# A search loop with its count turned on VectorE, its next choice moved into the gather, and transposes spread among products

## The chip, the cores and the metric

The kernel runs on one core of one Trainium2 chip. The metric is the time of one execution on the device in microseconds; of several runs the median is taken. The profile is of one more execution of the same program, taken by the hardware profiler.

## What is computed

The reference joins two blocks. The first is a linear attention without a softmax over 8 batches, 8 heads, 576 positions and head size 64: for each batch and head `kv = k^T v`, then `out = q kv`, divided by its root mean square over the head's 64 elements and scaled by `g_norm`. Its result is laid out as 4608 tokens of 512 elements.

The second is a mixture of 8 experts with a balanced choice. Each token has 8 logits (`x @ w_gate`). The pairs of token and expert are taken in falling order of their logits; a pair is granted if the token has no expert yet and the expert has fewer than 576 tokens. Then each expert computes `relu(x @ w1[e]) @ w2[e]` for its 576 tokens (512 to 1024 to 512 elements), and the rows go back to the tokens' places. All of it is float32.

## The kernel before

**Attention, lines 269 to 424.** The work goes batch by batch, two batches' loads ahead. Besides the outputs, each token's 8 logits and its inverse norm per head are computed; the tokens are written to a DRAM buffer `x_dram` (rows of 8 x 72 float32: a head's 64 elements, then the inverse norm and the logits). The logits lie in `lg`, [128 partitions, 8 experts, 36 columns]. `early` (269) makes the first choice and the first comparison for the columns as they become ready.

**The balanced choice, lines 234 to 262 and 437 to 542.** It is done in eight turns. In each turn one expert becomes full and is then computed. `choose` (234) finds each token's best open expert: `mx` is the logit, `best` a 0/1 tensor in bfloat16 that marks the expert. `threshold` (437) searches the logit at which the first expert becomes full: seven steps, each of which divides an interval into 33 parts. A step (i) makes 32 candidate levels (`candidates`, 259), (ii) compares every `mx` with each of them (`compare`, 254; `over` is [128, 36, 32]), (iii) counts, for each candidate and expert, the tokens above it: nine products on TensorE (`n_ps`, 453), each of four columns' `over` with the same columns' `best`, of whose result the four diagonal blocks are added on VectorE (459), (iv) decides for each candidate whether some expert is full (463, 466), (v) counts those candidates over the partitions with a product with ones (`k_ps`, 469), which puts the number on all 128 partitions, and (vi) picks the two candidates that bound the next interval (474, twice). `assign` (478) then settles who goes to the full expert. `fetch` (548) reads the expert's number on the SP engine, issues the loads of `w1` (two halves of 1 MB) and `w2` (2 MB), finds the row numbers of the 576 tokens (`a_ps`, `s_ps`, `ids`), gathers the tokens in five blocks with indirect DMAs on GpSimd (`xg`, 588) and works out the output rows (`outs`, 603). `later` (523) closes the expert. The last expert takes the rest (532).

**The experts, lines 619 to 677.** `turn` (619) scales the gathered tokens with the inverse norms on VectorE (`xs`, 625), transposes each block with four transposes on TensorE (629) and copies the result to `xt` on ScalarE (630); the buffers of `xs` and of the PSUM tile are two. `layers` (640) does the first layer in 16 groups of 288 tokens (four products each, 652; a float32 product stands as two records in the trace) and the second layer in five blocks of tokens, the last with 64 tokens (eight products, 663; 671).

**What sets the order.** TensorE, VectorE and ScalarE run in the order in which the program is written out; generators are interleaved by hand in lines 679 to 698. While `layers(t)` is written out, `control(t + 1)` is advanced: it yields how many microseconds of products, by the program's own numbers (0.487 for a first-layer product, 0.858 for a second-layer one), shall stand before its next TensorE instructions. When `layers` reaches its last block, the rest of `control` and the whole `turn(t + 1)` are written out.

## Time and profile before

| | us |
|---|---|
| Median of three runs | 751.49 |
| The three runs | 751.44, 751.49, 753.72 |
| The profiled execution | 748.19 |
| Its span, first to last instruction | 746.4 |
| TensorE busy with matmuls | 651.8 |
| VectorE busy | 352.6 |
| ScalarE busy | 162.9 |
| GpSimd busy | 92.9 |

All times inside the trace are counted from the start of the span; 748.19 is the span and 1.8 us around it. PE is TensorE's matmuls, PEld its weight loads, DVE VectorE, ACT ScalarE, POOL GpSimd, SP the engine that issues the loads; L469 is line 469. In a timeline a row has the start, the length to the end of the last of its instructions, engine, line, operation, output<-inputs, shapes (output<-input) and the number of instructions put together; in brackets stands the idle time before it and what ended that. In a table of groups the number behind the x counts instructions, then come busy us, the mean length of one in ns, and the engine's idle time before them. A matmul's length holds its way through the array, so the starts of successive ones are closer than their lengths. In a table of stretches the granted TensorE clock follows the engines, as a share of 2.4 GHz, then the busy share of the DMA engines and GB/s.

### The profile page before, as it was taken

Reading aid. Unit: us, or ns where it says so; the run is one execution under the profiler, and the core shown is the slowest. Engines: PE = TensorE matmul, PEld = TensorE weight load, DVE = VectorE, ACT = ScalarE, POOL = GpSimd, SP = SyncE. Lnnn points to the kernel's source line nnn. Section 1 sums busy time; section 2 is a strip of 40 time slices with the busy share of each in tenths; the row PEclk is TensorE's granted clock in tenths of the full one; section 3 lists DMA queues with packets and bytes.
Section 4 is the critical chain, followed back from the end, with each engine's and each line's share of the span. In section 5 each row is a group of like instructions: output and inputs, shape, how many; then the busy total and the mean of one; then the engine's idle time right before and its main releaser. Section 6 shows DMA issues by size and latency. Waiting matters only on the chain.

```text
span 746.4 us, 12251 instructions
## 1 busy us (share of the span) xinstructions
PE 651.8 (87%) x5001; PEld 412.3 (55%) x5001; DVE 352.6 (47%) x1253; ACT 162.9 (22%) x331; POOL 92.9 (12%) x113
## 2 busy tenths in 40 slices
PE   4788786114999999999999999999999999999994
PEld 3666674103764576457546744774476457547741
DVE  3444666785456465555645563655365542010000
ACT  1544555001110211031112112210211022122100
POOL 0100100002002300410040004001300322010011
PEclk9968996555999999999999999999999999999998
DMA  8997897017005400720090027004500638010001
GB/s 283 307 305 253 288 344 295 32 40 257 1 1 185 176 1 0 277 83 1 15 324 22 1 77 277 8 0 150 206 6 1 239 122 297 14 43 7 1 28 35
DMA packets 41399, 93.34 MB, mean 125 GB/s; under 512 B 3456, under 2 KB 3456, under 8 KB 41344
## 3 DMA queue, kind: packets, MB, share of 16 engines
q1 hardware_dynamic: 34752, 72.49, 27.8%
q0 software_dynamic: 5888, 20.06, 7.5%
q8 instruction: 39, 0.64, 0.3%
q10 hardware_dynamic: 704, 0.02, 0.1%
q14 instruction: 16, 0.13, 0.1%
HBM read 72.50 MB, written 20.05 MB: 124 GB/s over the span
## 4 chain that ended last, share of the span: by engine, by line
issue 60%; PE 19%; POOL 10%; DVE 6%; DMA 2%; ACT 1%; ACTq 0%; POOLq 0%; DVEq 0%
POOL out_dram L634 5%; PE h_ps L652 5%; POOL xg L588 5%; PE o_ps L359 3%; PE qt_ps L290 3%; PE kv_ps L302 3%; PE y_ps L663 2%; DVE over L255 1%; DMA gw<-in_moe_w_gate_dram 1%; DMA xg<-x_dram,ids 1%; PE w_ps L329 1%; PE n_ps L453 1%; DVE need L459 0%; DVE kv L310 0%; DVE at L474 0%
## 5 line engine op out<-in xcount | busy, mean ns | idle before, releaser
L652 PE MATMUL h_ps<-xt,w_sb 128*128 128x288 f32 x1024 | 272.2, 417 | 0.0
L663 PE MATMUL y_ps<-w_sb,hid 128*128 128x512 f32 x512 | 227.2, 597 | 0.0
L652 PEld LDWEIGHTS h_ps<-xt,w_sb 128*128 128x128 f32 x1024 | 189.6, 191 | 52.5 <-issue 5.7
L663 PEld LDWEIGHTS y_ps<-w_sb,hid 128*128 128x128 f32 x512 | 94.8, 190 | 105.2 <-issue 104.3
L655 ACT ACTIVATE hid<-h_ps 128x288 f32<-128x288 f32 x128 | 52.5, 410 | 221.4 <-PE h_ps L652 221.4
L634 POOL DMA_INDIRECT out_dram<-y_sb,outs x40 | 40.9, 1022 | 453.5 <-ACT y_sb L666 403.1
L625 DVE TENSOR_TENSOR xs<-xg 128x512 f32<-128x512 f32 (+1 forms) x40 | 27.1, 690 | 90.3 <-PE t_ps L629 45.8
L255 DVE TENSOR_TENSOR over<-mx,cand 128x1152 bf16<-128x1152 f32 (+3 forms) x52 | 67.5, 1298 | 1.6
L666 ACT COPY y_sb<-y_ps 128x512 f32<-128x512 f32 x32 | 18.7, 585 | 209.2 <-PE y_ps L663 209.2
L676 DVE TENSOR_TENSOR y_sb<-y_ps,y_part 64x512 f32<-64x512 f32 x8 | 5.5, 683 | 95.4 <-ACT y_part L675 95.4
L588 POOL DMA_INDIRECT xg<-x_dram,ids x40 | 38.9, 972 | 73.3 <-DVE at_row L598 37.0
L453 PEld LDWEIGHTS <-over 128*128 128x128 bf16 x441 | 18.1, 97 | 38.5 <-DVE over L255 19.7
L629 PE MATMUL t_ps<-ident,xs 128*128 128x128 f32 (+1 forms) x160 | 23.9, 284 | 16.6 <-DVE xs L625 13.0
L359 PE MATMUL o_ps<-kvx,qt 64*64 64x72 f32 x1152 | 33.4, 264 | 5.7 <-issue 4.9
L474 DVE SCALAR_TENSOR_TENSOR at<-row_f,k_ps,cand 128x33 f32<-128x33 f32 x98 | 21.5, 257 | 34.3 <-PE k_ps L469 34.3
L453 PE MATMUL n_ps<-best,over 128*128 128x32 bf16 x441 | 19.2, 178 | 20.9 <-DVE cand L447 12.5
L630 ACT ACTIVATE xt<-t_ps,g_col 128x512 f32<-128x512 f32 (+1 forms) x40 | 24.4, 646 | 51.8 <-PE t_ps L629 51.6
L459 DVE TENSOR_TENSOR need<-goal,n_ps 32x8 f32<-32x8 f32 x49 | 7.5, 154 | 58.5 <-PE n_ps L453 58.5
L290 PE MATMUL qt_ps<-ident,q_sb 128*128 128x128 f32 x144 | 30.5, 340 | 5.2 <-ACT kvt L323 2.0
L302 PE MATMUL kv_ps<-v_sb,k_sb 64*64 64x64 f32 x1152 | 28.6, 245 | 7.3 <-issue 7.3
L359 PEld LDWEIGHTS o_ps<-kvx,qt 64*64 64x64 f32 x1152 | 27.4, 164 | 11.7 <-issue 10.0
L367 DVE TENSOR_REDUCE ms<-sq 128x8 f32<-128x512 f32 x36 | 24.2, 681 | 18.4 <-ACT sq L365 18.4
(162 smaller groups left out, 472.8 us busy)
## 6 DMA issues: line engine op xcount, KB each, us to landing
w_sb<-in_moe_w_dram SPq DMA_DIRECT2D x16, 1024.0 KB, 6.2
w_sb<-in_moe_w_dram SPq DMA_DIRECT2D x8, 2048.0 KB, 16.2
k_sb<-in_k_dram SPq DMA_DIRECT2D x16, 576.0 KB, 6.1
v_sb<-in_v_dram SPq DMA_DIRECT2D x16, 576.0 KB, 5.8
q_sb<-in_q_dram SPq DMA_DIRECT2D x16, 576.0 KB, 4.8
x_dram<-o_sb SPq DMA_DIRECT2D x16, 576.0 KB, 4.1
x_dram<-o_sb SPq DMA_DIRECT2D x4, 288.0 KB, 3.4
xg<-x_dram,ids POOLq DMA_INDIRECT x40
```

The costliest lines, as they stand in the source:

```text
L255: nc.vector.tensor_tensor(over[:, c0:c1], mx[:, c0:c1].rearrange("p (c o) -> p c o", o=1).to_broadcast([P, c1 - c0, NCAND]), cand[:, 1:NCA ...
L290: nc.tensor.transpose(t_ps[:, x, :], q_sb[:, (4 * n + x) * P:(4 * n + x + 1) * P], ident)
L302: nc.tensor.matmul(kv_ps[cs, l, r * D:(r + 1) * D], lhsT=k_sb[ls, r, j, :], rhs=v_sb[ls, r, j, :], start=(j < 2), stop=(j >= R - 2))
L359: nc.tensor.matmul(o_ps[n * HP:(n + 1) * HP, rp, (2 * r2 + l) * W:(2 * r2 + l + 1) * W], lhsT=turned_q[bn][ks, block // 2, l * HP:(l + 1) ...
L453: nc.tensor.matmul(n_ps, lhsT=over[:, c:c + G].rearrange("p c n -> p (c n)"), rhs=best[:, c:c + G].rearrange("p c e -> p (c e)"), start=(c ...
L588: nc.gpsimd.indirect_dma_start(out=xg[0:nr].rearrange("p h w -> p (h w)"), out_offset=None, in_=x_dram, in_offset=bass.IndirectOffsetOnAxi ...
L625: nc.vector.tensor_tensor(xs[0:nr].rearrange("p (h d) -> p h d", h=H), xg[0:nr, :, 0:D], xg[0:nr, :, D:D + 1].to_broadcast([nr, H, D]), op ...
L630: nc.scalar.mul(xt[:, :, a:a + nr], t_ps[:, :, 0:nr], g_col)
L634: put = nc.gpsimd.indirect_dma_start(out=out, out_offset=bass.IndirectOffsetOnAxis(ap=ids_of[t][0:nr, n:n + 1], axis=0), in_=y_sb[0:nr, :] ...
L652: nc.tensor.matmul(h_ps, lhsT=w1[:, 2 * (d % 2) + d // 2, f * P:(f + 1) * P], rhs=xt[:, d, cs], start=(d == 0), stop=(d == DC - 1))
L655: nc.scalar.activation(hid[:, f, cs], h_ps, ACT.Relu)
L663: nc.tensor.matmul(y_ps, lhsT=hid[:, f, a:a + nr], rhs=w2[:, f, :], start=(f == 0), stop=(f == FC - 1))
```

## The change

- In `threshold`, the steps of the first search keep `k_ps`, but the lower end is picked first, the next candidates and the comparison follow, and then the upper end is picked. In all later searches `k_ps` is gone: the 0/1 decisions of 32 candidates are spread over 64 columns, turned in two 32 x 32 blocks on VectorE into `some_t` (which holds an added column of one and of zero), and summed there, which gives the count plus one and the count on 32 partitions; these are turned into the two ends directly and written to four groups of 32 partitions. The upper end is then limited by the one before.
- `best` is laid out as [expert, column]; `choose` writes it and `assign` reads it in a row, and the moving side of `n_ps` reads four columns of each expert.
- `choose` and the first comparison of the next search move from the start of `control` to the end of the one before, behind the issue of the gather (for the first expert, behind its `turn`).
- `turn` is advanced block by block: the first two blocks are scaled ahead; the transposes of four blocks stand after every second product of the second layer's fourth block, those of the fifth in the middle of the last block.
- The first expert's `w2` load waits for the last gather of its tokens.
- The yields are new numbers.

```diff
     away = asg.tile([P, NSTEP, NCAND + 1], FT, name="away")
+    part_of = [((1.0 + 2.0 ** -18) / (NCAND + 1)) ** (s + 1) for s in range(NSTEP)]
     for s in range(NSTEP):
         nc.vector.tensor_scalar(away[:, s], in0=row_f[:, 0:NCAND + 1], scalar1=span,
-                                scalar2=((1.0 + 2.0 ** -18) / (NCAND + 1)) ** (s + 1), op0=AL.mult, op1=AL.mult)
+                                scalar2=part_of[s], op0=AL.mult, op1=AL.mult)
+    some_t = asg.tile([QP, 2, QP + 1], FT, name="some_t")
+    nc.vector.memset(some_t[:, 0, QP:QP + 1], 1.0)
+    nc.vector.memset(some_t[:, 1, QP:QP + 1], 0.0)
     room = asg.tile([P, E], FT, name="room")
...
     pick = asg.tile([P, E, GC], FT, name="pick")
-    best = asg.tile([P, GC, E], BF, name="best")
+    best = asg.tile([P, E, GC], BF, name="best")
     mx = asg.tile([P, GC], FT, name="mx")
...
         nc.vector.tensor_reduce(code_mx[:, cs], pick[:, :, cs].rearrange("p e c -> p c e"), axis=AXX, op=AL.max)
-        nc.vector.tensor_tensor(best[:, cs].rearrange("p c e -> p e c"), pick[:, :, cs], bc_c(code_mx[:, cs]),
+        nc.vector.tensor_tensor(best[:, :, cs], pick[:, :, cs], bc_c(code_mx[:, cs]),
                                 op=AL.is_equal)
...
-    def threshold(first):
+    def threshold(first, over):
         lo, hi = bottom, top
+        cand = cand0
         for s in range(NSTEP):
-            if first and s == 0:
-                cand, over = cand0, over0
-            else:
-                cand = candidates(s, lo)
-                over = asg.tile([P, GC, NCAND], BF, name="over", tag="over", bufs=2)
-                compare(over, cand)
-                nc.vector.tensor_copy(cand[:, NCAND + 1:NCAND + 2], hi)
-            yield 7.2 if s == 0 else 2.8
-            n_ps = bank([P, G * E], "n_ps")
+            yield 0.4 if s == 0 else 4.6
+            lo_was = lo
+            n_ps = bank([P, E, G], "n_ps")
             for c in range(0, GC, G):
                 nc.tensor.matmul(n_ps, lhsT=over[:, c:c + G].rearrange("p c n -> p (c n)"),
-                                 rhs=best[:, c:c + G].rearrange("p c e -> p (c e)"),
+                                 rhs=best[:, :, c:c + G],
                                  start=(c == 0), stop=(c == GC - G))
...
                 less = small("need", E)[0:QP]
-                nc.vector.tensor_tensor(less, need, n_ps[g * QP:(g + 1) * QP, g * E:(g + 1) * E], op=AL.subtract)
+                nc.vector.tensor_tensor(less, need, n_ps[g * QP:(g + 1) * QP, :, g], op=AL.subtract)
                 need = less
...
             n_full = small("n_full")[0:QP]
-            nc.vector.scalar_tensor_tensor(full, in0=n_ps[0:QP, 0:E], scalar=0.0, in1=need, op0=AL.add,
+            nc.vector.scalar_tensor_tensor(full, in0=n_ps[0:QP, :, 0], scalar=0.0, in1=need, op0=AL.add,
                                            op1=AL.is_ge, accum_out=n_full)
-            some = small("some", dt=BF)[0:QP]
-            nc.vector.tensor_scalar(some, in0=n_full, scalar1=0.5, scalar2=None, op0=AL.is_gt)
-            yield 1.4
-            k_ps = bank([P, 1], "k_ps")
-            nc.tensor.matmul(k_ps, lhsT=ones_b[0:QP, :], rhs=some, start=True, stop=True)
+            hi_was = hi
             ends = small("ends", 2)
             hi, lo = ends[:, 0:1], ends[:, 1:2]
-            for n in range(2):
+            def pick_end(n):
                 at = small("at", NCAND + 1)
...
                                                op0=AL.is_equal, op1=AL.mult, accum_out=ends[:, 1 - n:2 - n])
+            if first:
+                some = small("some_b", dt=BF)[0:QP]
+                nc.vector.tensor_scalar(some, in0=n_full, scalar1=0.5, scalar2=None, op0=AL.is_gt)
+                k_ps = bank([P, 1], "k_ps")
+                nc.tensor.matmul(k_ps, lhsT=ones_b[0:QP, :], rhs=some, start=True, stop=True)
+                pick_end(0)
+            else:
+                some = small("some", 2 * QP)[0:QP]
+                nc.vector.tensor_scalar(some, in0=n_full.to_broadcast([QP, 2 * QP]), scalar1=0.5, scalar2=None, op0=AL.is_gt)
+                nc.vector.transpose(some_t[:, :, 0:QP], some.rearrange("p (t n) -> p t n", t=2))
+                kk = small("kk", 2)[0:QP]
+                nc.vector.reduce_sum(out=kk, in_=some_t, axis=AXX)
+                from_lo = small("from_lo", 2)[0:QP]
+                nc.vector.tensor_scalar(from_lo, in0=kk, scalar1=span[0:QP], scalar2=part_of[s], op0=AL.mult, op1=AL.mult)
+                for g in range(G):
+                    nc.vector.tensor_scalar(ends[g * QP:(g + 1) * QP], in0=from_lo, scalar1=lo_was[0:QP], scalar2=None, op0=AL.add)
+            if s + 1 < NSTEP:
+                cand_next = candidates(s + 1, lo)
+                over = asg.tile([P, GC, NCAND], BF, name="over", tag="over", bufs=2)
+                compare(over, cand_next)
+            if first:
+                pick_end(1)
+                if s + 1 < NSTEP:
+                    nc.vector.tensor_copy(cand_next[:, NCAND + 1:NCAND + 2], hi)
+                    cand = cand_next
+            else:
+                nc.vector.tensor_tensor(hi, hi, hi_was, op=AL.min)
         return ends
...
         for n in range(2):
-            nc.vector.tensor_tensor(two[:, n], best.rearrange("p c e -> p e c"), bc_c(cut[:, n]), op=AL.mult)
+            nc.vector.tensor_tensor(two[:, n], best, bc_c(cut[:, n]), op=AL.mult)
         sums = small("sums", 2 * E)
...
         nc.vector.tensor_copy(sums_b, sums)
-        yield 3.6
+        yield 5.4
         all_ps = bank([P, 3, E], "all_ps")
...
         w2 = wpool.tile([P, FC, DM], FT, name="w2_sb", tag="w2")
-        nc.sync.dma_start(w2, moe_w2[bass.ds(e, 1)].rearrange("o (a p) d -> p (o a) d", p=P))
+        w2_load = nc.sync.dma_start(w2, moe_w2[bass.ds(e, 1)].rearrange("o (a p) d -> p (o a) d", p=P))
         weights[t] = (w1, w2)
...
         nc.vector.tensor_tensor_scan(along, ones_b[:, 0:GC], own, 0.0, op0=AL.mult, op1=AL.add)
-        yield 5.5 if t < E - 1 else 8.0
+        yield 4.5 if t < E - 1 else 2.2
         a_ps = bank([P, GC + 1], "a_ps")
...
         nc.vector.tensor_scalar(since, in0=slot_f, scalar1=a_ps[:, 0:1], scalar2=None, op0=AL.is_ge)
-        yield 1.5
+        yield 1.6
         s_ps = bank([P, NB, GC + 3], "s_ps")
...
             xg = moe.tile([P, H, W], FT, name="xg", tag="xg", bufs=NB)
-            nc.gpsimd.indirect_dma_start(
+            tokens = nc.gpsimd.indirect_dma_start(
                 out=xg[0:nr].rearrange("p h w -> p (h w)"), out_offset=None, in_=x_dram,
...
             rows_of[t, n] = xg
+        if t == 0:
+            tc.add_manual_dep(w2_load.ins, tokens.ins.name,
+                              mybir.DependencyInfo(mybir.DependencyClass.Sync, mybir.DependencyReason.DATA),
+                              reason="TensorE waits for the tokens")
         up = asg.tile([P, NB, 2, GC], FT, name="up", tag="up")
...
         nc.vector.scalar_tensor_tensor(code_left, in0=code, scalar=which, in1=code_left, op0=AL.not_equal, op1=AL.mult)
+    compared = {0: over0}
     def control(t):
-        if t > 0:
-            choose()
         if t < E - 1:
-            which, index, later = yield from assign((yield from threshold(t == 0)))
+            which, index, later = yield from assign((yield from threshold(t == 0, compared.pop(t))))
         else:
...
         later()
+        if t == 0:
+            yield None
+        if t + 1 < E:
+            choose()
+        if t + 1 < E - 1:
+            compared[t + 1] = asg.tile([P, GC, NCAND], BF, name="over", tag="over", bufs=2)
+            compare(compared[t + 1], candidates(0, bottom))
     def turn(t):
...
         turned[t] = xt
-        for n, (a, nr) in enumerate(blocks):
+        scaled = []
+        def scale(n):
+            nr = blocks[n][1]
             xg = rows_of.pop((t, n))
...
                                     xg[0:nr, :, D:D + 1].to_broadcast([nr, H, D]), op=AL.mult)
+            scaled.append(xs)
+        scale(0)
+        scale(1)
+        yield
+        for n, (a, nr) in enumerate(blocks):
+            xs = scaled[n]
             t_ps = psm.tile([P, DC, P], FT, name="t_ps", tag="t")
...
             nc.scalar.mul(xt[:, :, a:a + nr], t_ps[:, :, 0:nr], g_col)
-            yield 0.5
+            if n + 2 < NB:
+                scale(n + 2)
+            yield
     def put(t, n, nr, y_sb):
...
         for n, (a, nr) in enumerate(blocks):
-            if n == NB - 1 and t + 1 < E:
-                yield None
             y_ps = psm.tile([P, DM], FT, name="y_ps", tag="y")
...
                     yield 0.858
+                    if n == NB - 2 and f % 2:
+                        yield None
                 nc.scalar.copy(y_sb, y_ps)
...
                     yield 0.858
+                    if f == 1:
+                        yield None
                 y_part = moe.tile([P // 2, DM], FT, name="y_part", tag="y_part")
...
     with tc.manual_schedule(engines={PE, DVE, ACTE}):
-        for _ in control(0):
+        ctl = control(0)
+        while next(ctl) is not None:
             pass
...
             pass
+        next(ctl, None)
         for t in range(E):
-            ctl = control(t + 1) if t + 1 < E else None
-            wait = next(ctl, None) if ctl is not None else None
+            ctl = control(t + 1) if t + 1 < E else iter(())
+            wait = next(ctl, None)
+            turning = None
             for used in layers(t):
-                if used is None:
+                if used is not None:
+                    if wait is not None:
+                        wait -= used
+                        if wait <= 0:
+                            wait = next(ctl, None)
+                elif t + 1 < E:
                     while wait is not None:
                         wait = next(ctl, None)
-                    for _ in turn(t + 1):
-                        pass
-                    continue
-                if wait is not None:
-                    wait -= used
-                    if wait <= 0:
-                        wait = next(ctl, None)
+                if wait is None and turning is None and t + 1 < E:
+                    turning = turn(t + 1)
+                    next(turning)
+                if used is None and turning is not None:
+                    next(turning)
 # ---- launch: one core; inputs and outputs as the reference has them ----
```

## Rows read from the trace of the kernel before

**Rows 1.** Stretches: from:to, length, busy (count) of PE, PEld, DVE, ACT, POOL, clock.

```profile
134.30:188.70 54.40, 15.43 (x104) 10.78 (x105) 38.02 (x145) 3.63 (x6) 4.89 (x5) 0.50 0.31 106
188.70:736.50 547.80, 542.38 (x2280) 323.09 (x2278) 241.06 (x902) 95.34 (x201) 73.97 (x74) 1.00 0.25 88
```

**Rows 2.** Timeline, TensorE, last expert: start us, length us, line, operation, count.

```profile
674.13 31.31 PE L652 MATMUL h_ps<-xt,w_sb 128*128 128x288 f32 x128
705.27 27.63 PE L663 MATMUL y_ps<-w_sb,hid 128*128 128x512 f32 x64
```

**Rows 3.** Timeline of TensorE, one round of a search beside an expert.

```profile
268.49 0.38 PE L453 MATMUL n_ps<-best,over 128*128 128x32 bf16 x9
268.72 1.70 PE L652 MATMUL h_ps<-xt,w_sb 128*128 128x288 f32 x6
270.36 0.17 PE L469 MATMUL k_ps<-some,ones_b 32*128 32x1 bf16 x1
270.46 3.18 PE L652 MATMUL h_ps<-xt,w_sb 128*128 128x288 f32 x12
273.47 0.28 PE L453 MATMUL n_ps<-best,over 128*128 128x32 bf16 x5
```

**Rows 4.** Groups of TensorE instructions, 183 to 737 us: busy, mean; idle before.

```profile
L469 PE MATMUL k_ps<-some,ones_b 32*128 32x1 bf16 x42 | 7.2, 172 | 0.0
...
L629 PE MATMUL t_ps<-ident,xs 128*128 128x128 f32 x112 | 15.9, 276 | 4.3 <-ACT xt L630 2.6 <-DVE xs L625 1.3 <-issue 0.3
```

**Rows 5.** Timeline of VectorE in the round of rows 3.

```profile
269.69 0.14 DVE L466 TENSOR_SCALAR some<-n_full 32x1 bf16<-32x1 f32 x1
270.57 0.26 DVE L474 SCALAR_TENSOR_TENSOR at<-row_f,k_ps,cand 128x33 f32<-128x33 f32 x1 [0.74 <-PE k_ps L469]
...
270.75 0.26 DVE L474 SCALAR_TENSOR_TENSOR at<-row_f,k_ps,cand 128x33 f32<-128x33 f32 x1
...
271.20 1.36 DVE L255 TENSOR_TENSOR over<-mx,cand 128x1152 bf16<-128x1152 f32 x1
```

**Rows 6.** Groups of VectorE instructions, 262 to 680 us: busy us, mean ns.

```profile
L249 DVE TENSOR_TENSOR best<-pick,code_mx 128x288 bf16<-128x288 f32 x5 | 7.2, 1448 | 0.2
...
L485 DVE TENSOR_TENSOR two<-best,cut 128x288 bf16<-128x288 bf16 x10 | 6.2, 668 | 0.2
...
L246 DVE TENSOR_TENSOR pick<-wl,mx 128x288 f32<-128x288 f32 x5 | 2.3, 458 | 0.2
```

**Rows 7.** Timeline of TensorE, 248 to 257 us: one expert's transposes.

```profile
249.18 1.04 PE L629 MATMUL t_ps<-ident,xs 128*128 128x128 f32 x8
...
252.55 3.65 PE L671 MATMUL y_ps<-w_sb,hid 128*64 128x512 f32 x16
```

**Rows 8.** Timeline, 237 to 262 us: from choice of tokens to scaling.

```profile
237.80 0.29 PE L574 MATMUL s_ps<-know,since 128*128 128x39 bf16 x5
...
239.48 0.17 DVE L585 SCALAR_TENSOR_TENSOR ids<-col,got 128x5 int32<-128x5 f32 x1
...
242.13 0.16 DVE L529 TENSOR_SCALAR shut<-is_full 128x8 f32<-128x8 f32 x1
...
246.46 0.69 DVE L625 TENSOR_TENSOR xs<-xg 128x512 f32<-128x512 f32 x1 [4.17 <-DMA xg<-x_dram,ids]
```

**Rows 9.** Timeline, 160 to 192 us: the last gather to the first products.

```profile
174.62 0.90 POOL L588 DMA_INDIRECT xg<-x_dram,ids  x1 [0.30 <-issue]
...
181.46 0.68 DVE L625 TENSOR_TENSOR xs<-xg 64x512 f32<-64x512 f32 x1 [0.88 <-DMA xg<-x_dram,ids]
...
182.88 9.45 PE L652 MATMUL h_ps<-xt,w_sb 128*128 128x288 f32 x26
...
186.41 1.36 DVE L255 TENSOR_TENSOR over<-mx,cand 128x1152 bf16<-128x1152 f32 x1
```

**Rows 10.** Part 6 of the page: DMA issues, KB each, median us to landing.

```profile
w_sb<-in_moe_w_dram SPq DMA_DIRECT2D x8, 2048.0 KB, 16.2
...
x_dram<-o_sb SPq DMA_DIRECT2D x4, 288.0 KB, 3.4
```

## The prediction

> **What bounds the kernel now.** I read the stages first. From 188.7 to 736.5 us TensorE is busy 542 of 547.8 us at a granted clock of 1.00 (2.4 GHz); in the 54.4 us before that it works for 15.4, at 0.50 (1.2 GHz) [rows 1]. So 73% of the span is a stretch in which only what TensorE itself issues counts, and before it stands a chain of small VectorE and DMA steps in which each link counts, up to the first product at 182.88 [rows 9]. Next I looked at what the expert stretch is made of. The last expert has no control beside it: 128 first-layer records in 31.31 us, 0.243 us each [rows 2]. A round of the search of another expert (lines 440 to 475) goes from 268.49 to 273.47, 4.98 us, of which 18 such records are 4.37; 0.61 us is what the round takes from TensorE [rows 3]. VectorE waits inside these rounds, 0.74 us before its picks alone [rows 5], and does not bound them. There are 42 rounds beside experts (six searches of seven), 42 k_ps products [rows 4].
>
> **The k_ps product goes (42 times).** The nine n_ps products take 0.23 us (268.49 to 268.72). The six records after them take 1.64 where 1.46 would do, 0.18 too much; k_ps takes 0.10 until the next record starts; the twelve records after it take 3.01 instead of 2.92, 0.09 too much [rows 3]. So a small product costs its own time and a disturbance on either side. The 0.09 behind k_ps is its own. The 0.18 lies between n_ps and k_ps; I give k_ps half. That makes 0.10 + 0.09 + 0.09, 0.28 to 0.29 us, and 42 x 0.29 = 12.2 us saved, all of it on the busy engine. Ends: 0.19 (all of the 0.18 stays with n_ps), 8.0 us; 0.37, 15.5 us.
>
> **Whether VectorE keeps up.** Its round becomes one chain between two n_ps groups: start of n_ps to start of some is 1.20 us (268.49 to 269.69) [rows 3, 5]; then come eight small instructions that no row shows in this form (some over 64 columns, the 32x32 turn, a sum over 66, from_lo, four writes of the ends), then cand and over. From the second pick at 270.75 to over is 0.45, of which 0.18 is that pick (270.57 to 270.75), so 0.27 for cand, and over takes 1.36 [rows 5]. For the first four I take 0.27 each (cand, 33 columns), 1.1 us; for four writes of two elements, 0.09 to 0.20 each, 0.8 at most. The round is 1.2 + 1.1 + 0.8 + 0.27 + 1.36, 4.7 us. The new yield of 4.6 lets ten first-layer products pass (0.487 each), and with n_ps the next group is due after 4.86 + 0.3 = 5.2 us. So 0.5 us to spare, and I cost the new chain at nothing: the products hide it. Without that cover each 0.1 us over is paid in 36 rounds, 3.6 us.
> The four writes go to four different groups of 32 partitions. The Trainium skill (VectorE: DVE Perf Modes, section "Two Vector instructions with no wait between them") says that an instruction whose output starts in another such group than the last one's is held until all earlier ones have finished; no run here shows such writes; by it they cost the upper 0.8 that is taken above, and the spare time is 0.5 instead of 0.9, which raises the chance of the second rival below.
>
> **n_ps reads best in strides.** best turns from [c, e] to [e, c], so the moving side of n_ps becomes eight runs of four bf16 and no longer 32 in a row. No row shows a strided moving operand. Bounds: nothing, or doubled, 42 x 0.23 = 9.7 us. I take nothing: a product of 32 columns is started 0.025 us after the last (nine in 0.23), a tenth of a record of 288 float32 columns. What strides can cost is seen on VectorE: writing best scattered takes 1.448 us where pick, of the same size, written in a row, takes 0.458 [rows 6]; this goes away.
> The Trainium skill (SBUF — State Buffer, the note on cachelines) says that 16-byte lines give full rate from two hits in a line on. The scattered write of best, one element to a line, agrees, 1.448 against 0.458; runs of four elements would still be free by it.
>
> **Turning the tokens (seven times).** Now all twenty transposes stand together, 249.18 to 252.55, 3.37 us [rows 7]. Their starts are 0.11 us apart inside a block (eight in 1.04, of which the last one's length is 0.276 [rows 4]), so 20 x 0.11 = 2.2 is work; the rest waits for ScalarE and VectorE, which empty and fill the buffers [rows 4]. With a block every second product, those waits lie beside 1.7 us of products. What is paid instead is a disturbance at five edges, 0.1 each by the row of k_ps: 2.7 us. Saved: 0.67 x 7 = 4.7 us. Ends: 0.2 at each edge, 3.2, which saves 1.2; no edges, 2.2, which saves 8.2.
> This needs xs earlier. A second-layer product is two records, 27.63 us for 32 of them, 0.86 [rows 2]. By the new yields s_ps comes after 5 + 6 + 2 = 13 of them instead of 20, 11.2 us behind the first. s_ps to ids is 1.7, ids to the first tokens 7.0 (one of six such places) [rows 8]: 19.9. VectorE is late as well, because choose and the first compare now stand before the scaling on the same engine: ids to the end of shut is 2.8 [rows 8], then 5.1 as worked out below, so it is free at 20.8 and has xs, 0.69 long, at 21.5. The first transposes are due after 26 products, 22.3. Spare: 0.8. The expert weights load beside this as now, only earlier. The out-row puts that wait behind the gathers on POOL's queue have four buffers.
>
> **The first expert's chain.** Six times the second pick leaves the chain, 0.18 each, 1.1 us [rows 5]; reading best in a row shortens the two of 0.668 us, which I bound by the 0.458 of a float32 pair: 0.4 [rows 6]. The w2 load of 2 MB is issued before the gathers; the last gather, issued at 174.62, is used at 181.46, 6.8 us later [rows 9]. Held back, it leaves the gathers beside w1 alone. Ends for that gather: 6.8 as now, or 3.4, what a write of 288 KB takes to land without weights beside it [rows 10]; I take 3.4, because w1 is the first half of 4 MB that take 16 us [rows 10], through by 174. Gain 3.4. w2 then lands, at half of those 16 us, some 8 us behind the gathers, and is needed 31 us after the first product; behind it SP's queue has nothing until the next expert's weights.
> Against that stands a new wait. The search of the second expert starts with a yield of 0.4: n_ps is due after one product, 1.7 us behind the last scaling (182.14 to 182.88, and 0.97 for two records at half clock). But choose and compare only follow that scaling on VectorE. They end now at 187.77, 5.6 us behind it [rows 9]. best in a row is 0.99 shorter [rows 6], but VectorE starts the next instruction before the last one's length is over (0.26 long, 0.18 to the next [rows 5]), so I take 0.6 of it: 5.1. TensorE waits 3.4 us. The granted clock is 0.50 up to 188.7 [rows 1], and an idle stretch there will not bring it up sooner; I let it rise as long after the restart as it now does after the start. Stage: -1.1 - 0.4 - 3.4 + 3.4 = -1.5 us; ends -4.9 (no wait) and +1.9 (the gather as late as now).
>
> **Sum.** -12.2 - 4.7 - 1.5 = -18.4 us. The profiled execution took 748.19 us (span 746.4), 3.3 below the median of 751.49: 729.8 by its own time, 733.1 against the median.
>
> **Rivals.**
> 1. The tokens come late. For it: the gathers share the DMA with 4 MB of weights, xs has 0.8 us to spare, and in the order written out for TensorE a late block now stops 8.6 us of second-layer work that used to run first. Against: choose stands in that time too, so the tokens may land 0.9 us later before VectorE waits for them, and 1.7 before TensorE does. 0.5 to 1 us of wait in six experts: 736 to 739.
> 2. The new chain does not fit, and the kernel is slower. Place: between n_ps and the next n_ps, on VectorE. It decides from a round of 5.2 + 18.4 / 36 = 5.7 us on. Were each of the eight small instructions to cost 0.458, as 288 elements do [rows 6], the round would be 1.2 + 3.7 + 0.27 + 1.36 = 6.5, 1.3 over, 36 x 1.3 = 47 us: 780. Against: they hold 2 to 66 elements each, and the pick of 33 takes 0.18 to the next [rows 5].
> 3. The strided read doubles n_ps: 9.7 us beside the experts and 1.6 in the first search, 744.
> 4. The change does less than it says: the disturbance stays with n_ps and only 0.10 goes with k_ps, 4.2 us instead of 12.2: 741.
>
> **Chances.** Forecast 0.62 (728 to 737), tokens late 0.17, chain too long 0.06, strided read 0.06, smaller k_ps 0.09. The range goes from the best ends of the turn and of the first stage (3.5 and 3.4 us below, most of both) to rivals 1 and 4 with 2 us over, 727 to 743, and leaves out rivals 2 and 3 and a little below. A measurement of this kernel tells about 0.3% from no change. Slower by more than that: most of rival 2, 0.04. Within: the mild ends of rivals 1 and 2 together with the poor ends of the sums, 0.03. Faster: 0.93.
>
> **What would show it.** A round beside an expert: n_ps to n_ps 5.2 us with 20 records, no k_ps, no TensorE idle before n_ps. The twenty transposes in five groups, none with TensorE idle before it. From one expert's first product to the next one's 2.7 us less than now (7 x 0.29 + 0.67). The first product near 178 us, then a gap of 3 to 4 us before the first n_ps, released by over. Wrong if n_ps waits for over in every round (rival 2), if transposes wait for xs (rival 1), if n_ps starts come over 0.025 us apart (rival 3), or if a round takes 0.5 us and not 0.3 beyond its records (rival 4).

## The result, and the profile after

The changed kernel takes 733.32 us (median of 4 runs, 728.39 to 734.3) beside 751.47 for the kernel before (4 runs, 749.29 to 753.72): ratio 0.9733, 95% interval 0.9683 to 0.9783. In a later session it took 730.98 beside 749.78, 0.9744 (0.9701 to 0.9787). Forecast: 733.1, 727 to 743, faster. The profiled executions are 748.19 and 728.39 us, 19.8 apart. From start to start of the experts' first products, that difference lies here:

| stretch | before, us | after, us | difference |
|---|---|---|---|
| start to the first product of expert 1 | 182.88 | 178.36 | -4.5 |
| expert 1 | 73.26 | 72.71 | -0.6 |
| experts 2 to 6, together | 352.11 | 337.94 | -14.2 |
| expert 7 (no search beside it) | 65.88 | 65.31 | -0.6 |
| expert 8 to the last instruction | 72.3 | 72.3 | 0.0 |

The stretches of the kernel after, split where the clock rises; columns as in [rows 1]:

```profile
128.90:186.90 58.00, 15.72 (x113) 10.61 (x114) 45.02 (x175) 3.87 (x7) 5.74 (x6) 0.50 0.33 109
186.90:716.70 529.80, 528.95 (x2230) 321.01 (x2228) 281.47 (x1014) 96.83 (x201) 76.29 (x74) 1.00 0.26 91
```

TensorE still bounds the long stretch and now has under 1 us of it free. VectorE's share of it rose from 44% [rows 1] to 53% (281.47 of 529.80). So the saving there must be work that TensorE no longer does or waits that it no longer has. First a round of a search, on TensorE (answers to [rows 3]):

```profile
319.24 0.38 PE L452 MATMUL n_ps<-best,over 128*128 128x32 bf16 x9
...
324.69 0.39 PE L452 MATMUL n_ps<-best,over 128*128 128x32 bf16 x9
324.93 5.10 PE L704 MATMUL h_ps<-xt,w_sb 128*128 128x288 f32 x20
329.86 0.31 PE L452 MATMUL n_ps<-best,over 128*128 128x32 bf16 x6
```

From 324.69 to 329.86 it is 5.17 us with twenty records, and 5.16 in the rounds that follow: 0.30 beyond the records (0.2433 each), where it was 0.60. The same round on VectorE (answers to [rows 5]):

```profile
325.89 0.18 DVE L482 TENSOR_SCALAR some<-n_full 32x64 f32<-32x64 f32 x1
...
326.87 0.92 DVE L490 TENSOR_SCALAR ends<-from_lo,ends 32x2 f32<-32x2 f32 x4
327.83 0.24 DVE L265 TENSOR_SCALAR cand<-away,ends 128x33 f32<-128x33 f32 x1
328.11 1.36 DVE L259 TENSOR_TENSOR over<-mx,cand 128x1152 bf16<-128x1152 f32 x1
```

The chain from n_ps (324.69) to the end of over (329.47) is 4.78 us, and the next n_ps is due at 329.86: it fits. The first round of each search from the third expert's on is longer, 5.45 (319.24 to 324.69). VectorE's list there shows two causes:

```profile
319.38 0.68 DVE L730 TENSOR_TENSOR y_sb<-y_ps,y_part 64x512 f32<-64x512 f32 x1 [6.23 <-ACT y_part L729]
...
320.88 0.37 DVE L482 TENSOR_SCALAR some<-n_full 32x64 f32<-32x64 f32 x1
```

The last sum of the expert before starts just as n_ps does, so some begins 1.64 us behind the start of n_ps instead of 1.20; and some itself takes 0.37 instead of 0.18. The chain is 5.39 long, 0.61 more than in the other rounds. In all five such rounds some ends within 0.01 us of the end of GpSimd's issue of the expert's last output rows (L685, 321.25 here). Whether it waits for that was not tried. Next, the transposes of one expert (answers to [rows 7]):

```profile
239.94 0.60 PE L678 MATMUL t_ps<-ident,xs 128*128 128x128 f32 x4
240.37 1.88 PE L713 MATMUL y_ps<-w_sb,hid 128*128 128x512 f32 x4
242.09 0.60 PE L678 MATMUL t_ps<-ident,xs 128*128 128x128 f32 x4
...
246.41 0.60 PE L678 MATMUL t_ps<-ident,xs 128*128 128x128 f32 x4
246.94 1.94 PE L723 MATMUL y_ps<-w_sb,hid 128*64 128x512 f32 x8
248.80 0.46 PE L678 MATMUL t_ps<-ident,xs 64*128 64x64 f32 x4
```

No group waits. Start to start (before rounding) the groups take 0.44, 0.44, 0.44 (the one left out), 0.53 and 0.39, 2.23 us in all, where the block took 3.37; four times 0.11 is 0.44, so the first three cost nothing at their edges. Between them, four records of y_ps take 1.72 (240.37 to 242.09), as four of the 64 in [rows 2] do. The split last block does cost something: 0.09 in the group ahead of it (0.53), and its two halves take 1.86 each (246.94 to 248.80), 3.73 where the whole block took 3.58 before (252.55 to 256.13). That is 0.23 in all. The saving is 1.0 us for this expert and 0.95 for the later ones, whose block took 3.33 before; one block took 3.77 (at 460.23) and saves 1.4.

The first stage (answers to [rows 9]):

```profile
167.46 1.15 POOL L614 DMA_INDIRECT xg<-x_dram,ids  x1 [35.88 <-DVE at_row L628]
...
172.98 1.23 POOL L614 DMA_INDIRECT xg<-x_dram,ids  x1 [0.31 <-issue]
...
176.38 0.37 SPq L582 DMA_DIRECT2D w_sb<-in_moe_w_dram  x1
176.50 0.68 DVE L667 TENSOR_TENSOR xs<-xg 64x512 f32<-64x512 f32 x1
...
178.36 1.33 PE L704 MATMUL h_ps<-xt,w_sb 128*128 128x288 f32 x2
...
180.66 1.36 DVE L259 TENSOR_TENSOR over<-mx,cand 128x1152 bf16<-128x1152 f32 x1
...
182.08 0.42 PE L452 MATMUL n_ps<-best,over 128*128 128x32 bf16 x9 [2.40 <-DVE over L259]
```

The last gather is issued 1.64 us earlier and its tokens are used 3.5 us after the issue instead of 6.84, without a wait, right behind the scaling of the block before; w2 is issued behind it. The first product starts 4.5 us earlier, and then TensorE stands for 2.40 us, because n_ps waits for over. The clock is at 0.50 up to 186.9, 4.8 us after that restart.

### The profile page after: what moved, and what is told of

It reads as the page before. It is cut to its first block, busy times and chain, and to the rows that moved or that the text cites. A ratio compares the mean times of both kernels' runs of the same rounds, so it can differ in the third digit from the quotient of the medians.

```text
span 726.6 us, 12295 instructions
## 1 busy us (share of the span) xinstructions
PE 632.7 (87%) x4959; PEld 404.6 (56%) x4959; DVE 395.3 (54%) x1381; ACT 164.4 (23%) x331; POOL 95.8 (13%) x113
## 4 chain that ended last, share of the span: by engine, by line
PE 62%; issue 19%; DVE 11%; POOL 2%; ACT 2%; DMA 2%; ACTq 0%; POOLq 0%; DVEq 0%
PE y_ps L713 23%; PE h_ps L704 23%; PE y_ps L723 3%; PE qt_ps L294 3%; PE o_ps L363 3%; PE kv_ps L306 3%; DVE over L259 2%; PE t_ps L678 2%; PE n_ps L452 2%; POOL out_dram L685 1%; POOL xg L614 1%; DMA gw<-in_moe_w_gate_dram 1%; DVE need L458 1%; DVE ms L371 1%; DVE ends L490 1%
## 5 line engine op out<-in xcount | busy, mean ns | idle before, releaser
L704 PE MATMUL h_ps<-xt,w_sb 128*128 128x288 f32 x1024 | 264.1, 414 | 0.0
L704 PEld LDWEIGHTS h_ps<-xt,w_sb 128*128 128x128 f32 x1024 | 191.9, 192 | 54.9 <-issue 5.7
L685 POOL DMA_INDIRECT out_dram<-y_sb,outs x40 | 42.9, 1073 | 427.7 <-ACT y_sb L718 399.4
L363 PE MATMUL o_ps<-kvx,qt 64*64 64x72 f32 x1152 | 30.9, 247 | 10.8 <-issue 9.9
L678 PEld LDWEIGHTS t_ps<-ident,xs 128*128 128x128 f32 (+1 forms) x160 | 19.6, 150 | 30.6 <-issue 23.1
L363 PEld LDWEIGHTS o_ps<-kvx,qt 64*64 64x64 f32 x1152 | 25.0, 149 | 16.6 <-issue 14.8
L306 PE MATMUL kv_ps<-v_sb,k_sb 64*64 64x64 f32 x1152 | 27.1, 235 | 7.5 <-issue 7.5
L490 DVE TENSOR_SCALAR ends<-from_lo,ends 32x2 f32<-32x2 f32 x144 | 31.6, 219 | 2.8
```

The lines of the kernel that those rows point to most:

```text
L306: nc.tensor.matmul(kv_ps[cs, l, r * D:(r + 1) * D], lhsT=k_sb[ls, r, j, :], rhs=v_sb[ls, r, j, :], start=(j < 2), stop=(j >= R - 2))
L363: nc.tensor.matmul(o_ps[n * HP:(n + 1) * HP, rp, (2 * r2 + l) * W:(2 * r2 + l + 1) * W], lhsT=turned_q[bn][ks, block // 2, l * HP:(l + 1) ...
L490: nc.vector.tensor_scalar(ends[g * QP:(g + 1) * QP], in0=from_lo, scalar1=lo_was[0:QP], scalar2=None, op0=AL.add)
L678: nc.tensor.transpose(t_ps[:, d, 0:nr], xs[0:nr, d * P:(d + 1) * P], ident[0:nr, 0:nr])
L685: put = nc.gpsimd.indirect_dma_start(out=out, out_offset=bass.IndirectOffsetOnAxis(ap=ids_of[t][0:nr, n:n + 1], axis=0), in_=y_sb[0:nr, :] ...
L704: nc.tensor.matmul(h_ps, lhsT=w1[:, 2 * (d % 2) + d // 2, f * P:(f + 1) * P], rhs=xt[:, d, cs], start=(d == 0), stop=(d == DC - 1))
```

## The experiments

e5 to e8 ran once each, beside 745.78 us for the kernel before; of them the profile is read. The others ran several times.

**Is a k_ps product worth 0.30 us?** A product of the same form is put back where it does no work: between the tenth and the eleventh record (the fifth and the sixth product) of 36 rounds (e1_extra_mid), or directly behind n_ps (e2_extra_beside).

```diff
-            yield 0.4 if s == 0 else 4.6
+            if s == 0:
+                yield 0.4
+            else:
+                yield 2.3
+                if not first:
+                    nc.tensor.matmul(bank([P, 1], "d_ps"), lhsT=ones_b[0:QP, :], rhs=ones_b[0:QP, 0:1], start=True, stop=True)
+                yield 2.3
```

> The changed kernel with a product of the form of k_ps put back in the middle of each round but the first of a search (36 in all), which nothing waits for; ten first-layer products per round as before. Theory (a small product costs its own 0.10 us and about 0.09 to 0.10 on either side): a round goes from 5.16 to 5.46 us, an expert with six of them from 67.59 to 69.4, the kernel from 733.3 to about 744. Rival (the disturbance belongs to n_ps and stays with it): 0.10 each, 68.2 us per expert, 737.

Measured: 739.58 us, 0.9874 of before (0.9793 to 0.9956). One round, on TensorE:

```profile
329.70 0.38 PE L458 MATMUL n_ps<-best,over 128*128 128x32 bf16 x9
329.93 2.67 PE L710 MATMUL h_ps<-xt,w_sb 128*128 128x288 f32 x10
332.53 0.17 PE L451 MATMUL d_ps<-ones_b 32*128 32x1 bf16 x1
332.63 2.69 PE L710 MATMUL h_ps<-xt,w_sb 128*128 128x288 f32 x10
335.16 0.38 PE L458 MATMUL n_ps<-best,over 128*128 128x32 bf16 x9
```

The round is 5.46 and no longer 5.16: 0.30, though the product itself takes 0.10 to the next start. The period from expert to expert grows by 1.50, five rounds of it; in the first round the product lies inside the wait that is there already (5.45 to 5.46). So the price is that of the product, for which nothing waits.

```diff
                                  start=(c == 0), stop=(c == GC - G))
+            if not first and s > 0:
+                nc.tensor.matmul(bank([P, 1], "d_ps"), lhsT=ones_b[0:QP, :], rhs=ones_b[0:QP, 0:1], start=True, stop=True)
             need = goal[0:QP]
```

> The same 36 extra products, but directly behind the nine of n_ps. Theory (what costs is the change from float32 products to small ones and back, so that a small product beside another shares the edges): 0.03 to 0.10 us each, 67.8 to 68.2 us per expert, 734 to 737. Rival (each small product costs 0.3 wherever it stands): 69.4 us per expert, 744.

Measured: 738.37 us, 0.9872 (0.9773 to 0.9972). Neither number came: the rounds are 5.37, +0.21.

```profile
330.44 0.39 PE L452 MATMUL n_ps<-best,over 128*128 128x32 bf16 x9
330.76 0.17 PE L456 MATMUL d_ps<-ones_b 32*128 32x1 bf16 x1
330.86 5.12 PE L706 MATMUL h_ps<-xt,w_sb 128*128 128x288 f32 x20
335.81 0.35 PE L452 MATMUL n_ps<-best,over 128*128 128x32 bf16 x8
```

Ahead of it 0.32 instead of the 0.24 that n_ps takes to the next start, itself 0.10, and the twenty records behind 4.95 instead of 4.93. What is missing against e1 is the price behind the product, which n_ps pays there anyway. The price ahead and its own stay in either place.

**What in the product is dear?** The new theory was its form, weights of 32 rows. e5_mid_128_rows is e1 with weights of 128 rows.

```diff
-                    nc.tensor.matmul(bank([P, 1], "d_ps"), lhsT=ones_b[0:QP, :], rhs=ones_b[0:QP, 0:1], start=True, stop=True)
+                    nc.tensor.matmul(bank([P, 1], "d_ps"), lhsT=ones_b, rhs=ones_b[:, 0:1], start=True, stop=True)
```

> As the first of these runs (36 extra products in the middle of the rounds, nothing waits for them), but with weights of 128 rows instead of 32. Theory, new after the extra product beside n_ps took 0.21 us (0.085 in front of it that the row before does not have, 0.10 of its own): the dear part of k_ps is its form with 32 rows, and a product of 128 rows costs 0.03 of its own and 0.08 behind it, as a_ps does: rounds of 5.27 us, 68.1 us per expert. Rival (any small product between large ones costs 0.30): rounds of 5.46, 69.1 us per expert.

Measured: 736.07 us, rounds 5.27.

```profile
330.40 2.67 PE L710 MATMUL h_ps<-xt,w_sb 128*128 128x288 f32 x10
332.91 0.17 PE L451 MATMUL d_ps<-ones_b 128*128 128x1 bf16 x1
332.94 2.67 PE L710 MATMUL h_ps<-xt,w_sb 128*128 128x288 f32 x10
```

Ahead 2.51 instead of 2.60, itself 0.03 instead of 0.10: a small product of this form costs 0.11. The weight loads show where the two forms part, first with 32 rows (e1), then with 128 (e5):

```profile
332.53 0.09 PEld L451 LDWEIGHTS <-ones_b 32*128 32x128 bf16 x1 [0.39 <-issue]
```

```profile
332.67 0.10 PEld L451 LDWEIGHTS <-ones_b 128*128 128x128 bf16 x1
```

With 128 rows the load starts 0.24 us ahead of its product (332.91), while the record before still runs; with 32 rows it starts only with the product (332.53), after 0.39 without a load. k_ps has the same 0.39 in the kernel before. Why this load does not start ahead, no run shows. The last test of this is on the kernel before, e11_before_k128: its own k_ps, 128 rows instead of 32, the 96 other rows of the moving column zero.

```diff
+    some_z = [asg.tile([P, 1], BF, name=f"some_z{n}") for n in range(2)]
+    for z in some_z:
+        nc.vector.memset(z, 0.0)
...
-            some = small("some", dt=BF)[0:QP]
-            nc.vector.tensor_scalar(some, in0=n_full, scalar1=0.5, scalar2=None, op0=AL.is_gt)
+            some = some_z[s % 2]
+            nc.vector.tensor_scalar(some[0:QP], in0=n_full, scalar1=0.5, scalar2=None, op0=AL.is_gt)
...
-            nc.tensor.matmul(k_ps, lhsT=ones_b[0:QP, :], rhs=some, start=True, stop=True)
+            nc.tensor.matmul(k_ps, lhsT=ones_b, rhs=some, start=True, stop=True)
```

> The kernel before, with its k_ps product given 128 rows of weights instead of 32 (the moving column is held in one of two columns that are zero below row 32), nothing else changed; its vector chain, order and yields are those of before. Theory (0.20 of the 0.30 us that a k_ps product cost came from its 32-row weights, as the extra product with 128 rows, 0.11, against the one with 32, 0.30, says): a round beside an expert from 4.98 us to 4.78 (two rounds' records being 18), 42 x 0.20 = 8.4 us in all, 0.989 of before, about 741 beside a before of 749. Rival (the 0.20 belongs to that extra product alone, whose operands were constants; k_ps waits for VectorE's some and keeps its price in any form): rounds 4.98, same time as before, 1.000.

Measured: 742.6 us, 0.9903 (0.9875 to 0.9932), rounds 4.79 where it was 4.98.

```profile
267.07 0.38 PE L457 MATMUL n_ps<-best,over 128*128 128x32 bf16 x9
267.30 1.70 PE L656 MATMUL h_ps<-xt,w_sb 128*128 128x288 f32 x6
268.84 0.17 PE L473 MATMUL k_ps<-some_z,ones_b 128*128 128x1 bf16 x1
268.87 3.16 PE L656 MATMUL h_ps<-xt,w_sb 128*128 128x288 f32 x12
271.86 0.38 PE L457 MATMUL n_ps<-best,over 128*128 128x32 bf16 x9
```

Beside [rows 3]: 1.54 instead of 1.64 ahead of k_ps, 0.03 instead of 0.10 for it, 2.99 instead of 3.01 behind. Some 0.19 of the 0.30 us was the form, and the wider slice, with zeros under the moving column, takes 7 us off the kernel before. By that sum, taking the product away altogether is worth the other 0.11 a round, 4.6 us.

**The count by k_ps again, in the new order** (e3_k_back): every search counts by the product, 3.2 and 1.4 of yields instead of 4.6.

```diff
-            yield 0.4 if s == 0 else 4.6
+            yield 0.4 if s == 0 else 3.2
...
+                yield 1.4
                 k_ps = bank([P, 1], "k_ps")
...
-            which, index, later = yield from assign((yield from threshold(t == 0, compared.pop(t))))
+            which, index, later = yield from assign((yield from threshold(True, compared.pop(t), t)))
```

> The changed kernel with the count done by k_ps in every search, seven products behind it and three in front, ten per round as in the changed kernel; everything else is kept. Theory (the gain of the search is the missing product): 42 x 0.30 = 12.6 us back, 746 in all, 69.7 us per expert. Rival (the gain came from ten products per round and the new places, not from the product): at most 4 us back, at most 68.3 us per expert.

Measured: 750.98 us, 1.002 (0.9976 to 1.0065): nothing of the gain is left. Rounds 5.46 as in e1, but the periods are 70.6 to 70.9, +3.0 to +3.3 and not +2.1, and the rest has a line of its own:

```profile
386.64 0.66 PE L682 MATMUL t_ps<-ident,xs 128*128 128x128 f32 x4 [1.25 <-DVE xs L671]
```

The choice of tokens comes two second-layer products later here, and the first transposes wait for the tokens: the first rival of the prediction, in a kernel where its condition holds. Counted by starts the wait is 1.4, and 6 x 0.30 + 1.4 is 3.2 of the 3.28 that this period (70.87) gained.

**The transposes together again** (e4_turn_together), in front of the split last block.

```diff
-                    if n == NB - 2 and f % 2:
-                        yield None
...
+            if n == NB - 1:
+                yield None
...
-                    next(turning)
+                    for _ in turning:
+                        pass
```

> The changed kernel with all five blocks' transposes in one place again, in front of the last block of the second layer; the first two blocks are still scaled ahead. Theory (the gain of the spreading is the waits for ScalarE and VectorE between blocks): a gap of about 3.3 us for the twenty transposes instead of 2.24 and 0.14 in pieces, 0.95 x 7 = 6.6 us back, 68.6 us per expert, 740 in all. Rival (the pieces pay as much at their edges as they hide, my 0.1 to 0.2 per edge): 1 to 5 us back.

Measured: 738.33 us, 0.9842 (0.9768 to 0.9917); the period grows by 0.93.

```profile
387.58 1.04 PE L678 MATMUL t_ps<-ident,xs 128*128 128x128 f32 x8
389.05 1.23 PE L678 MATMUL t_ps<-ident,xs 128*128 128x128 f32 x8 [0.44 <-ACT xt L679]
...
390.91 1.51 PE L723 MATMUL y_ps<-w_sb,hid 128*64 128x512 f32 x6
```

3.33 us again, with the waits for ScalarE. So the spreading alone is worth 0.93 x 7 = 6.5 us.

**Four more steps in VectorE's chain** (e7_four_more_steps): four copies of kk before from_lo.

```diff
+                for x in range(4):
+                    k2 = small(f"kx{x}", 2)[0:QP]
+                    nc.vector.tensor_copy(k2, kk)
+                    kk = k2
```

> The changed kernel with four copies of two elements, each waiting for the last, between the sum and from_lo in every round of the later searches (42 x 4). Theory (VectorE's chain of 4.8 us is hidden with 0.3 to 0.4 us to spare, and each 0.1 over is paid): four steps of 0.20 to 0.25 are 0.8 to 1.0, rounds of 5.16 become 5.6 to 5.8, n_ps waits for over in each of them, 17 to 24 us more. Rival (VectorE is not what a round waits for even then): rounds of 5.16.

Measured: 748.92 us; rounds 5.60, and n_ps waits.

```profile
334.21 0.39 PE L452 MATMUL n_ps<-best,over 128*128 128x32 bf16 x9 [0.89 <-DVE over L259]
```

This is the first round of a search, with the longest wait. The copies take 0.76 us in the chain and the rounds grow by 0.43: 0.33 us were spare. The second rival's mechanism is there, but it needs a chain 0.33 longer than that of the change, which is two such copies (0.19 each).

**The next choice back in front of the search** (e8_choose_back).

```diff
     def control(t):
+        if t > 0:
+            choose()
+            if t < E - 1:
+                compared[t] = asg.tile([P, GC, NCAND], BF, name="over", tag="over", bufs=2)
+                compare(compared[t], candidates(0, bottom))
...
-        if t + 1 < E:
-            choose()
-        if t + 1 < E - 1:
-            compared[t + 1] = asg.tile([P, GC, NCAND], BF, name="over", tag="over", bufs=2)
-            compare(compared[t + 1], candidates(0, bottom))
...
-            yield 0.4 if s == 0 else 4.6
+            yield 7.2 if s == 0 else 4.6
```

> The changed kernel with choose and the first comparison at the start of each search again, behind a yield of 7.2 as before; the transposes stay where they are now. Theory (moving them is what makes room for the early transposes): s_ps comes 8 second-layer products later, the first transposes wait some 5 us for xs in six experts, 72 to 73 us per expert, about 760 in all; in the first expert n_ps does not wait for over. Rival (the tokens have room enough): 67.3 to 67.6 us per expert.

Measured: 776.75 us, periods 74.9 to 75.5, some 2.5 more than expected. On TensorE, and (columns as in [rows 1]) one stretch:

```profile
395.21 1.11 PE L678 MATMUL t_ps<-ident,xs 128*128 128x128 f32 x4 [5.34 <-DVE xs L667]
396.12 3.62 PE L713 MATMUL y_ps<-w_sb,hid 128*128 128x512 f32 x4
...
640.28 0.16 PE L590 MATMUL a_ps<-along,before 128*128 128x1 bf16 x1 [3.44 <-DVE along L587]
```

```profile
392.80:399.60 6.80, 4.39 (x9) 2.22 (x10) 2.07 (x3) 0.69 (x1) 2.63 (x3) 0.50 0.85 307
```

The wait for the tokens costs 5.34, and inside it the granted clock falls to 0.50 and stays there until 399.6, 4.4 us after work came back. At that level four transposes take 0.91 instead of 0.44 and four records of y_ps 3.62 instead of 1.88 (240.37 above): 2.2 us more, 7.5 in all. All six such waits, 5.34 to 6.29, brought the fall. The shorter ones of e3 and e7 did not, nor did the 3.44 before a_ps in the last row.

**w2 not held** (e6_w2_free): the added dependency of the w2 load is left out.

```diff
-        if t == 0:
+        if False:
             tc.add_manual_dep(w2_load.ins, tokens.ins.name,
```

> The changed kernel with the first w2 load not held back. Theory (w2 shares the DMA with the gathers): the last block of tokens is scaled about 3.4 us later behind its issue, and the first product and all that follows come 3.4 us later; the wait for over stays. Rival (the gathers are as fast as POOL can issue them): under 1 us.

Measured: 732.62 us, the later periods as in the changed kernel.

```profile
169.00 1.15 POOL L614 DMA_INDIRECT xg<-x_dram,ids  x1 [35.89 <-DMA w_sb<-in_moe_w_dram]
...
182.34 1.33 PE L704 MATMUL h_ps<-xt,w_sb 128*128 128x288 f32 x2
```

Executions differ in when this stage begins, so I count from the issue of the first gather to the first product: 13.46 before (from 169.42), 13.34 here, 10.90 in the changed kernel (from 167.46). Holding w2 is worth 2.4 us, less than the 3.4 expected and more than the rival's 1. From the issue of the last gather it would be 2.75 (8.13 to 5.38), but with w2 held that gather itself is issued 0.3 later behind the first.

**A later first count** (e9_first_wait, e10_first_waits_all). If only the order is at fault for the 2.40 us, n_ps can be asked for later: in the second expert's search after 2.0 and then every 4.3; in e10 also after 0.9 in the first rounds of the other searches, with 5.2 instead of 5.4 behind their last. The diff is that of e10; e9 has 0.4 in place of the 0.9 and leaves the 5.4.

```diff
-            yield 0.4 if s == 0 else 4.6
+            yield (2.0 if t == 1 else 0.9) if s == 0 else 4.3 if t == 1 and s > 1 else 4.6
...
-        yield 5.4
+        yield 5.2
```

> The changed kernel with the yields of the second expert's search alone changed: 2.0 instead of 0.4 ahead of the first n_ps, 4.3 instead of 4.6 from the third on. Theory (TensorE stands still there for over and its clock rises the later for it): no wait ahead of the first n_ps, the clock up about 6 us after the first product instead of 8.5, 2 to 3 us less from the first expert's first product to the second's (72.7 to about 70), five rounds with about 0.1 us of wait; 731 in all. Rival (the clock rises by its own time and the wait lies at half speed anyway): at most 1 us less.

Measured: 727.97 us, 0.9736 (0.9699 to 0.9773); first expert 69.75 and no longer 72.71. TensorE, and the stretch up to the rise of the clock:

```profile
177.88 3.97 PE L704 MATMUL h_ps<-xt,w_sb 128*128 128x288 f32 x10
182.09 0.39 PE L452 MATMUL n_ps<-best,over 128*128 128x32 bf16 x9 [0.24 <-DVE over L259]
```

```profile
129.00:180.50 51.50, 12.23 (x98) 8.47 (x99) 39.30 (x157) 3.50 (x6) 5.91 (x6) 0.50 0.38 126
```

Ten records stand where the wait was, and the clock rises 2.6 us after the first product; in the changed kernel it was 8.5, of which 2.4 without work. The rounds asked for every 4.3 come every 4.83 (the first of them 4.82), each n_ps some 0.14 late: VectorE's chain of 4.78 and 0.06 to the next n_ps, read once more. The moment of the rise is not chance alone: in the eight profiled executions that have a wait of 2.4 to 2.9 us ahead of this n_ps (the changed kernel and e1 to e7) it lies 8.5 to 9.8 us behind the first product, in the five that have none or next to none (before, e8, e9, e10, e11) 2.6 to 5.8.

> As the last one, and in all later searches 0.9 instead of 0.4 ahead of the first n_ps and 5.2 instead of 5.4 behind the last. Theory (the first round of each search is 0.2 to 0.3 us long because VectorE first adds the last block's two halves): the first rounds go from 5.45 to 5.17, 67.3 us per expert instead of 67.6, about 1.5 us less than the last one, 729.5 in all. Rival (the round is long for another reason): 67.6.

Measured: 726.69 us, 0.9709 (0.9677 to 0.9742): first rounds 5.16, periods 67.29, first expert 69.66. For a narrower comparison the changed kernel ran again:

> The changed kernel itself, unaltered, for a narrower interval beside the same kernel before as the two versions with first waits (0.9736 and 0.9709 of before). Theory (those waits gain what their traces show: 3.0 us in the first expert and 0.3 in each of five later periods, 4.4 in all, 0.6%): the changed kernel at 0.976 to 0.978 of before, 731 to 733 beside 749. Rival (the first expert's 3 us belong to the moment at which the clock rises in one execution, so only 1.5 us are gained): 0.972 to 0.974, 728.5 to 730. Expected of the profile: rounds 5.16, first rounds of a search 5.45, period 67.59; the first n_ps of the second expert's search released by over after some 2.4 us without work on TensorE.

Measured: 730.98 us, 0.9744 (0.9701 to 0.9787), between what the two theories say and nearer to the second; rounds and periods came out as expected, the first wait at 2.86. The traces are on the first one's side: the first expert took 72.71 and 72.97 (e6) with the wait, 69.75 and 69.66 without it. e10 is the fastest version: by its traces 0.30 us less in five periods and 3 us in the first expert, by the medians 4 us. The intervals of the two ratios overlap, so how much of this a run keeps is not settled.

## Why the prediction was right

- **k_ps: size right, reason too general.** "a small product costs its own time and a disturbance on either side": 0.29 was forecast, 0.30 measured, 42 x 0.302 = 12.7 us for 12.2, and e1 finds the same 0.30 for a product put back. Giving half of the 0.18 ahead to k_ps was right too: with the product gone the round keeps 0.30, what n_ps takes with its own disturbance behind. But e5 and e11 show that 0.19 of it comes with weights of 32 rows; a small product as such costs 0.11. The [rows 3] hold no second form to compare with.
- **VectorE keeps up: right.** 4.7 us forecast; 4.78 by its rows, 4.83 from n_ps to n_ps where it sets the round (e9); 0.33 spare by e7, 0.5 forecast. To the start of some 1.20, as worked out; the eight small instructions 1.94 for 1.9. The four writes take 0.23 from start to start, a little over their length of 0.22: none overlaps the one before. That is the upper price. By the Trainium skill (VectorE: DVE Perf Modes, "Two Vector instructions with no wait between them") a write whose output starts in another group of 32 partitions than the last one's is held until the earlier ones have finished, and the trace agrees.
- **Strided reads: right.** Nine n_ps in 0.23 to 0.24, as in [rows 3]. Rival 3 is out. Of the reads and writes in a row, best takes 0.462 on average (1.448 in [rows 6]) and the two of L485, now L511, 0.304 each, less than the 0.458 of the bound:

```profile
L511 DVE TENSOR_TENSOR two<-best,cut 128x288 bf16<-128x288 bf16 x10 | 2.6, 304 | 0.2
```

- **Transposes: the step that was mis-sized.** "a disturbance at five edges, 0.1 each by the row of k_ps": 0.23 was measured, all of it around the split last block, and nothing at the other groups. The end "no edges" (8.2 saved) was nearer: 1.0, five times 0.95 and once 1.4 make 7.1 us instead of 4.7. The row of k_ps was the wrong neighbour: it is a bf16 product with weights of 32 rows, and the transposes are float32 with 128, like the products around them. Which of the two differences counts for them was not tried.
- **Tokens in time: right, and close.** over ends at 238.20, the first xs at about 238.8, the transposes start at 239.94: 1.1 us to spare for the 0.8 worked out. e3, two products later, waits 1.25, and e8, with the choice in front of the search, 5.34.
- **First stage: sum right by luck, links off.** First product -4.5 (forecast -4.9). Of this, 0.75 is there already at the first count of the first search (127.22 and 126.47), a moment that lies anywhere from 126.1 to 131.4 in the profiled executions of the changed kernel and its variants e1 to e10, so it cannot be put down to the change. The chain up to the gather gains 1.2, not 1.5: a first-search round is 0.06 shorter without the second pick (3.68 to 3.62) and not 0.18, the first 0.22, the two reads in a row give 0.7 and not 0.4. From the first gather to the first product it is 2.6 instead of 3.4. The last gather's tokens are used 3.3 us sooner after the issue, as forecast, but right behind the block before, and then two xs and their transposes stand in line. The new wait is 2.40 instead of 3.4 (2.75 counted from when n_ps was due, as the forecast does), since the first product starts 1.2 us behind the last xs and the choice takes 4.9. The clock rose 4.8 us after the restart, 5.8 were assumed; the eight executions with this wait have 4.4 to 5.8. Against a saving of some 3.1 us (seven times 0.302 and 1.0), expert 1 saved 0.6, so 2.5 went there, and the change gains about 1.2 in the stage for 1.5.
- **What was missed:** the longer first round of five searches, 0.29 each, 1.5 us, by the add at its head and a slower some. Neither row stands among those read; in e10 the first n_ps was moved to behind the add, and the rounds are 5.16.

In expert 7, which saved 0.6 where 0.95 was due, a_ps is asked for earlier than before and waits for VectorE:

```profile
591.90 0.16 PE L590 MATMUL a_ps<-along,before 128*128 128x1 bf16 x1 [0.21 <-DVE along L587]
```

By starts that is 0.4. Then -12.7 - 7.1 + 1.5 - 1.2 - 0.75 + 0.4 is -19.9, against -19.8 between the profiled executions (-18.4 forecast). That the median came out 0.2 us from the 733.1 is in part luck: the turn brought 2.4 us more than forecast, and the 1.5 of the first rounds was in no term. Rival 4 is out: a round keeps 0.30 beyond its records, not 0.5.

## What to carry to other kernels

Price a small product by the distance between its neighbours, less their own work, and not by its length; then try it in the form of those neighbours before moving it to another engine: in this kernel a wider slice of the weights, with zeros under the moving column, gave 7 of the 18 us. Transposes of the type of the products around them cost little more than their starts here, once their inputs were early. After a change of order, look at the first item of every loop: what sits in front of it on each engine is not what sits in front of the others.

## What was not expected of the hardware

- A bf16 product with 32-row weights among float32 products with 128 rows: 0.30 us between them, 0.21 directly behind other bf16 products, against 0.11 with 128 rows. The load of its weights started with the product itself, that of 128 rows 0.24 us ahead of it.
- Groups of four float32 transposes among float32 products: 0.11 for each transpose, nothing at the edges, except around the last block of 64 tokens (0.23).
- After 5.34 us without work in a stretch at full clock, the grant was 0.50 for 6.8 us; after waits of up to 3.44 us it stayed at 1.00.
- With work coming with hardly a gap, the time from the first product to the full clock was 5.8 us before, 4.8 in e11, 4.0 in e8, 2.9 in e10 and 2.6 in e9. Why it differs was not tried.
